# Accumulator banks of a blocked MLP: four half-used banks packed in two, four banks for first products, the output chain on DVE, eight products for the last two items

## The chip, the cores and the metric

The kernel runs on one core of one Trainium2 chip. A core has five engines that run their own instruction streams and wait for each other by semaphores: TensorE (PE in the profile; its weight loads are PEld), VectorE (DVE), ScalarE (ACT), GpSimd (POOL) and SyncE (SP), which here only issues DMAs. The metric is device time in microseconds (us) of one execution; lower is better. Before the change it is 464.85 us, the median of three runs (464.08 to 465.17).

## The reference: what is computed

One block of a network over x of 2048 rows (tokens) by 512 columns. A small conditioning vector c gives six modulation rows (shift, scale and gate for each half). In numpy's words, cut to what matters:

```
mod = (silu(c) @ w_mod).reshape(1, 6, 1, 512)
sa, ca, ga, sb, cb, gb = mod[:, 0], ..., mod[:, 5]
h = layernorm(x) * (1 + ca) + sa
x = x + ga * irfft2(rfft2(h) * (w_r + 1j * w_i))
h = layernorm(x) * (1 + cb) + sb
a = mish(h @ w1 + b1)                  # 512 -> 1376, mish(z) = z * tanh(softplus(z))
x = x + gb * (a @ w2)                  # 1376 -> 512
```

The change is in the last three lines, the MLP, which takes the last two thirds of the kernel's time. All is float32; the products on TensorE run on float32 numbers that are split in a high and a low part.

## The kernel before, in words

**Stages.** The kernel first does the spectral part: forward transform, multiplication by the filter, backward transform (the functions p1_..., p2_..., p3_...). The backward transform's last step, p3_row, adds its result to x, which stays in SBUF as 16 tiles of 128 rows. While that loop (s from 0 to 16) runs, w1 and parts of w2 are loaded and split, and the statistics for the second layernorm are taken tile by tile (norm_sums). norm_scale turns the statistics of four tiles into 1/std by a logarithm and an exponential on ACT and four short steps on DVE.

**The MLP's items.** The 2048 rows are 8 blocks (NB) of 256 rows, and the 1376 hidden columns are cut in 6 items per block (NT): item 0 has one tile of 96 hidden columns, items 1 to 5 have two tiles of 128 each. There are so 48 items, numbered s in the code. For each:

- up: first products. Each tile of hidden columns fills one PSUM bank of 128 x 512 floats, by four products 512 wide (L722) and four 256 wide (L724).
- mish: ACT adds the bias to one half of the bank (L732) and DVE adds the other half (L733); this add is the bank's last reader. Then comes Mish on ACT (L735). For a two-tile item DVE forms four sums and differences (L745), since the second products use a scheme of seven instead of eight products for two halves of rows by two halves of hidden columns.
- high and low: the seven operands are rounded to their high part on ACT (L755, two casts) and the rest is taken on DVE (L761, two subtractions).
- down: second products. Seven products of 256 columns, each as three matmuls (high by high, high by low, low by high; TERMS), so 21 matmuls (L784); item 0 has six matmuls 512 wide (L770). They add up over the items of a block.

down lags two items behind (LAG): TensorE's order is up(s), transposes if any, down(s - 2). The order on every engine is the order in which the program's text issues the instructions (tc.manual_schedule).

**Banks.** PSUM has eight banks here, as four names (A, B, C, D) of two. First products of the MLP take A (two banks), so tile one of item s waits until the add L733 of item s - 1 has read its bank. The transposes of the next block's rows (transpose_in, in items 4 and 5) also take A. The six sums of a block take C, B, B, C, D, D; the tables RAW, SUM and END say which product goes into which bank and half. Four of these six banks use only 256 of 512 columns.

**Output chain.** After the block's last down, in item 1 of the next block, gather copies the four half-used banks to SBUF with ACT (L791). own_rows reads the two full banks with DVE (L796, L797). chain then combines these on POOL (L802 to L819: five additions and two products by the gate gb), add_rows adds them to x on POOL (L824), and store writes two tiles with one DMA each. In the last block the chain runs on DVE and the last item uses plain eight products, whose w2 tile is loaded anew and split by plain_w2.

**Next block's rows.** norm_pair normalizes two tiles on ACT in item 3 (L141), transpose_in turns them in items 4 and 5, and split_in scales, rounds (ACT, L624, L628) and subtracts (DVE, L629). The next block's first products need all of it.

Of the kernel before, what the change touches and what calls it, by code (L numbers as in the profile page):

```python
# [23 lines left out]
RAW = ((0, None, 0, 0), (1, 0, 2, 1), (2, 0, 1, 6))  # L24
SUM = ((3, None, 3, 3), (4, None, 4, 4), (5, None, 5, 5), (1, 1, 6, 2))
# [5 lines left out]
def tile_spectral_block(ctx: ExitStack, tc: tile.TileContext, x_d, w1_d, b1_d, w2_d,  # L31
# [668 lines left out]
    def plain_w2():  # L700
        w2["plain"] = [w.rearrange("p e d -> p (e d)") for w in w2[1]]
        h, l = w2["plain"]
        for e, r in enumerate(st.pop(("w2", 5))):
            split(h[:, 512 * e:512 * e + 512], l[:, 512 * e:512 * e + 512], r)
# [9 lines left out]
    def up(g):  # L714
# [3 lines left out]
        for e, f, rows in tiles(t):  # L718
            ps = bank("C" if g < 2 and e == 0 else "A")[:rows]
# [7 lines left out]
    def mish(g):  # L727
# [9 lines left out]
        if g == total - 1:  # L737
# [25 lines left out]
    def down(g):  # L763
        b, t = divmod(g, NT)
        a = acts.pop(g)
        if t == 0:
            out_ps[b] = out = [bank(n) for n in "CBBCDD"]
# [5 lines left out]
        if g == total - 1:  # L773
            for n, half in ((2, 0), (1, 1)):
                for f in range(2):
                    for i, (p, q) in enumerate(TERMS):
                        nc.tensor.matmul(out[n], a[p][:, half + 2 * f], w2["plain"][q][:, 512 * f:512 * f + 512],
                                         start=False, stop=(f == 1 and i == 2))
            return
        for n, half, e, r in END if g == total - 2 else RAW + SUM:  # L780
            o = out[n][:, 0:256] if half is None else out[n][:, 256 * half:256 * half + 256]
            last = t == 5 or (half is None and g == total - 2)
            for i, (p, q) in enumerate(TERMS):
                nc.tensor.matmul(o, a[p][:, e], w2[t][q][:, r], start=(half is None and t == 1 and i == 0),  # L784
                                 stop=(last and i == 2 and (n, half) != (1, 0)))

    def gather(b):
        out = out_ps[b]
        p, q = buf("h"), buf("h")
        for o, k in ((p[:, 0:256], 0), (q[:, 0:256], 4), (q[:, 256:], 5), (p[:, 256:], 3)):  # L790
            nc.scalar.copy(o, out[k][:, 0:256])  # L791
        done[b] = p, q

    def own_rows(b):
        r = buf("y"), buf("y")
        nc.vector.tensor_tensor(r[1], out_ps[b][1], done[b][0], op=ALU.add)  # L796
        nc.vector.tensor_copy(r[0], out_ps[b][2])  # L797
        return r

    def chain(b, eng, r):  # L800
        p, q = done.pop(b)
        eng.tensor_tensor(q[:, 0:256], q[:, 0:256], p[:, 0:256], op=ALU.add)  # L802
        eng.tensor_tensor(q[:, 256:], q[:, 256:], q[:, 0:256], op=ALU.add)
        both = q[:, 256:].unsqueeze(1).to_broadcast([P, 2, 256])
        v = r[0].rearrange("p (j d) -> p j d", j=2)
        if b == NB - 1:
            eng.tensor_copy(v, both)
        else:
            eng.tensor_tensor(v, v, both, op=ALU.add)
        eng.tensor_tensor(r[0][:, 256:], r[0][:, 256:], p[:, 256:], op=ALU.add)  # L810
        if b == NB - 1:
            eng.tensor_tensor(r[1][:, 256:], p[:, 256:], q[:, 0:256], op=ALU.add)
            eng.tensor_tensor(r[1][:, 0:256], p[:, 0:256], gbr[:, 0:256], op=ALU.mult)
            eng.tensor_tensor(r[1][:, 256:], r[1][:, 256:], gbr[:, 256:], op=ALU.mult)
            eng.tensor_tensor(r[0], r[0], gbr, op=ALU.mult)
        else:
            eng.tensor_tensor(r[1][:, 256:], r[1][:, 256:], q[:, 0:256], op=ALU.add)
            for t in r[::-1]:
                eng.tensor_tensor(t, t, gbr, op=ALU.mult)  # L819

    def add_rows(b, eng, r, rows=(1, 0)):
        for i in rows:
            n = 2 * b + i
            eng.tensor_tensor(x[:, n, :], x[:, n, :], r[i], op=ALU.add)  # L824

    def store(b, rows=(1, 0)):
        for r in rows:
            n = 2 * b + r
            nc.sync.dma_start(ov[:, n:n + 1, :], x[:, n:n + 1, :])
# [4 lines left out]
    def mlp(s):  # L834
# [20 lines left out]

    def finish():
        b = NB - 1
        down(total - 2)
        gather(b)
        r = buf("y"), buf("y")  # L860
        chain(b, nc.vector, r)
        add_rows(b, nc.vector, r)
        down(total - 1)
        for i in range(2):
            nc.vector.tensor_tensor(r[i], out_ps[b][2 - i], gbr, op=ALU.mult)
            add_rows(b, nc.vector, r, (i,))
            store(b, (i,))
# [8 lines left out]
    for s in range(N2 + 1):  # L876
# [26 lines left out]
        if s in (7, 8):  # L903
            split_in(0, s - 7)
    low(high(0, mish(0)))
# [4 lines left out]
    for s in range(LAG, total):  # L910
# [9 lines left out]
        if s == 2 * NT + 2:  # L920
# [142 lines left out]
```

## Time and profile before

| | |
|---|---|
| median of three runs | 464.85 us (464.08 to 465.17) |
| profiled execution | 464.28 us, of which the span of the trace is 462.5 |
| busy, share of the span | PE 88%, PEld 80%, DVE 68%, ACT 56%, POOL 35% |
| mean granted TensorE clock | 0.966 |
| MLP's first product | at 154.26 us |
| last product | ends at 455.58 us |

A row of the timeline has the start, the duration, the engine, the line and the operation, the tile written and the tiles read, the shapes and how many instructions are merged (x4). A bracket gives the idle time of that engine before it and the instruction that ended it. A row of the windows has, for each engine, the busy time and the number of instructions, then the TensorE clock that was granted (1.00 is full speed), the share of DMA and GB/s. A group of the lines has the busy time in all, the mean of one in ns, and the idle time before. L numbers are lines of the kernel before.

### The profile page before, as it was taken

To read this page: it belongs to the slowest core of one execution; us is meant where nothing else is said; L and a number is where in the kernel's file an instruction comes from. 1 tells how busy PE (TensorE), PEld (TensorE's weight loads), DVE (VectorE), ACT (ScalarE), POOL (GpSimd) and SP (SyncE) were. 2 spreads that over 40 slices of the span, in tenths; PEclk is the share of its full clock that TensorE was granted. 3 is DMA by queue.
4 is the path that set the end of the run, shared out by engine and by line. 5 is a ranking of instruction groups with operands and counts; after the bars stand their busy time and mean duration, and the time that the engine had idled before them with its cause. 6 is when DMAs were issued, how large, how long until landed. Compare 5 with 4: busy or idle time off the path is not lost.

```text
span 462.5 us, 7587 instructions
## 1 busy us (share of the span) xinstructions
PE 407.9 (88%) x2800; PEld 369.5 (80%) x2800; DVE 312.8 (68%) x620; ACT 259.5 (56%) x563; POOL 159.6 (35%) x188
## 2 busy tenths in 40 slices
PE   8999899999999997978985997998798799699694
PEld 7888678998999887867874985887787688688593
DVE  2999786862899867585466539547655764853966
ACT  1778646666496576636547643653654464464261
POOL 0776446560566122080053008007104302600800
PEclk9999999999999999997998899899899899999998
DMA  8999814622134101000001000000100100100111
GB/s 278 354 345 327 300 58 133 247 79 91 50 120 123 40 26 46 1 22 24 0 1 46 1 0 30 18 1 0 47 1 1 45 1 0 47 0 1 39 54 45
DMA packets 20900, 35.21 MB, mean 76 GB/s; under 512 B 3712, under 2 KB 6560, under 8 KB 20480
## 3 DMA queue, kind: packets, MB, share of 16 engines
q1 hardware_dynamic: 20432, 34.21, 21.8%
q10 hardware_dynamic: 432, 0.53, 0.3%
q8 instruction: 22, 0.36, 0.3%
q14 instruction: 14, 0.11, 0.1%
HBM read 30.53 MB, written 4.19 MB: 75 GB/s over the span
## 4 chain that ended last, share of the span: by engine, by line
PE 44%; DVE 32%; ACT 16%; issue 4%; DMA 2%; POOL 1%; SPq 0%; DVEq 0%; ACTq 0%; POOLq 0%
PE bank L784 12%; PE bank L722 12%; PE bank L724 6%; DVE buf L745 5%; DVE al L761 4%; DVE st L112 4%; ACT ah L755 3%; DVE buf L733 3%; PE bank L456 3%; PE bank L502 2%; DVE ve L125 2%; ACT buf L735 2%; ACT buf L141 2%; DVE x L650 2%; ACT buf L791 2%
## 5 line engine op out<-in xcount | busy, mean ns | idle before, releaser
L745 DVE TENSOR_TENSOR buf<-buf 128x128 f32<-128x128 f32 x156 | 62.5, 441 | 29.4 <-ACT buf L735 27.4
L761 DVE TENSOR_TENSOR al<-buf,ah 128x512 fp32r<-128x512 f32 (+2 forms) x87 | 65.5, 779 | 18.1 <-ACT ah L755 15.8
L755 ACT CAST ah<-buf 128x512 fp32r<-128x512 f32 (+2 forms) x87 | 46.0, 550 | 46.8 <-DVE buf L745 32.1
L722 PE MATMUL bank<-h2e,w1h 128*128 128x512 f32 (+1 forms) x176 | 53.3, 424 | 18.0 <-DVE buf L733 16.4
L722 PE MATMUL bank<-h2o,w1h 128*128 128x512 f32 (+1 forms) x176 | 53.3, 423 | 17.7 <-DVE buf L733 15.4
L802 POOL TENSOR_TENSOR buf<-buf 128x256 f32<-128x256 f32 x7 | 5.2, 744 | 183.1 <-ACT buf L791 183.1
L732 ACT ACTIVATE buf<-bank,b1n 128x256 f32<-128x256 f32 (+1 forms) x88 | 40.4, 472 | 43.7 <-PE bank L724 43.7
L733 DVE TENSOR_TENSOR buf<-buf,bank 128x256 f32<-128x256 f32 (+1 forms) x88 | 35.3, 416 | 38.6 <-ACT buf L732 38.4
L735 ACT ACTIVATE buf<-buf 128x512 f32<-128x512 f32 (+1 forms) x48 | 28.6, 597 | 44.7 <-DVE buf L733 44.6
L722 PEld LDWEIGHTS bank<-h2e,w1h 128*128 128x128 f32 (+1 forms) x176 | 31.6, 199 | 26.1 <-DVE buf L733 18.9
L722 PEld LDWEIGHTS bank<-h2o,w1h 128*128 128x128 f32 (+1 forms) x176 | 31.5, 199 | 26.1 <-DVE buf L733 18.0
L784 PE MATMUL bank<-w2a,ah 128*128 128x256 f32 x168 | 36.9, 286 | 0.0
L784 PE MATMUL bank<-w2b,ah 128*128 128x256 f32 x161 | 34.3, 283 | 0.0
L724 PEld LDWEIGHTS bank<-h2o,w1l 128*128 128x128 f32 (+1 forms) x176 | 29.1, 202 | 4.5
L724 PEld LDWEIGHTS bank<-h2e,w1l 128*128 128x128 f32 (+1 forms) x176 | 29.0, 201 | 4.6
L724 PE MATMUL bank<-h2o,w1l 128*128 128x256 f32 (+1 forms) x176 | 30.1, 297 | 0.0
L724 PE MATMUL bank<-h2e,w1l 128*128 128x256 f32 (+1 forms) x176 | 30.0, 296 | 0.0
L784 PEld LDWEIGHTS bank<-w2a,ah 128*128 128x128 f32 x168 | 28.1, 192 | 0.0
L784 PEld LDWEIGHTS bank<-w2b,ah 128*128 128x128 f32 x161 | 26.8, 191 | 0.0
L112 DVE BATCH_NORM_STATS2 st<-x 128x6 f32<-128x512 f32 x32 | 22.0, 688 | 4.9 <-DMA x<-in_A_x_dram 4.5
L637 PE MATMUL bank<-kc,d 128*128 128x128 f32 x128 | 24.8, 276 | 0.5 <-ACT d L360 0.5
L234 PE MATMUL bank<-buf,mring 128*128 128x512 f32 x48 | 21.4, 446 | 4.2 <-DVE buf L227 1.9
(210 smaller groups left out, 1054.7 us busy)
## 6 DMA issues: line engine op xcount, KB each, us to landing
buf<-in_B_w_dram SPq DMA_DIRECT2D x20, 256.0 KB, 2.7
xring<-in_x_t_dram SPq DMA_DIRECT2D x16, 256.0 KB, 4.8
x<-in_A_x_dram SPq DMA_DIRECT2D x16, 256.0 KB, 5.1
wm<-in_w_mod_dram SPq DMA_DIRECT2D x16, 256.0 KB, 4.3
out_dram<-x SPq DMA_DIRECT2D x16, 256.0 KB, 2.0
mraw<-in_km_dram SPq DMA_DIRECT2D x16, 128.0 KB, 4.9
wqa<-in_w_q_dram SPq DMA_DIRECT2D x8, 256.0 KB, 4.3
wqb<-in_w_q_dram SPq DMA_DIRECT2D x8, 256.0 KB, 4.6
```

What stands on the lines that cost most here:

```text
L112: nc.vector.bn_stats(t, x[:, n, :])
L234: nc.tensor.matmul(pa, m[:, a, 0:128], g, start=(i == 0), stop=False)
L637: nc.tensor.matmul(o, dj[:, 0:128], kc[0][:, n, :], start=True, stop=False)
L722: nc.tensor.matmul(ps, w1h[:, k, fs], h[:, k], start=(k == 0), stop=False)
L724: nc.tensor.matmul(ps[:, 0:256], w1l[:, k, fs], h[:, k, 0], start=False, stop=(k == 3))
L732: nc.scalar.activation(o, ps[:, 256:], AF.Identity, bias=b1n[:rows, f:f + 1])
L733: nc.vector.tensor_tensor(o, o, ps[:, 0:256], op=ALU.add)
L735: nc.scalar.activation(o, o, AF.Mish)
L745: nc.vector.tensor_tensor(o, p, q, op=op)
L755: nc.scalar.copy(h, r)
L761: nc.vector.tensor_tensor(l, r, h, op=ALU.subtract)
L784: nc.tensor.matmul(o, a[p][:, e], w2[t][q][:, r], start=(half is None and t == 1 and i == 0), stop=(last and i == 2 and (n, half) != (1, 0)))
```

## The change

- The four half-used sums share two banks: sums 0 and 3 are two halves of one bank, 4 and 5 of another. A block's sums take C, B, B, C. Only the first product into such a bank carries the start flag.
- First products take A for an item's first tile and D for its second, so four banks in turn; the transposes take A and D likewise (items of the first block before it: C and D).
- In item 1 of a block the order becomes up, Mish, down of the last block's item 5, gather (two copies 512 wide), then the casts of high; before, the casts came ahead of gather.
- The output chain runs on DVE: four steps (chain) ahead of low's subtractions and four (residual) behind them, the last two 1024 wide over both tiles; POOL has nothing of it. One DMA stores both tiles.
- norm_scale of the last four tiles moves from item 2 of block 2 to just ahead of the first Mish.
- The last two items, not one, use eight plain products; their w2 tiles are loaded anew (two more DMAs) and split into the places of w2 items 1 and 2. down_last runs the 24 products 512 wide for both items at the end, the even rows' bank first. finish combines the block's other sums on ACT, DVE and POOL while they run.

```diff
-RAW = ((0, None, 0, 0), (1, 0, 2, 1), (2, 0, 1, 6))
-SUM = ((3, None, 3, 3), (4, None, 4, 4), (5, None, 5, 5), (1, 1, 6, 2))
+RAW = ((0, 0, 0, 0), (1, 0, 2, 1), (2, 0, 1, 6))
+SUM = ((0, 1, 3, 3), (3, 0, 4, 4), (3, 1, 5, 5), (1, 1, 6, 2))
...
-        st["pt2", g] = ps = bank("A" if n else "D")
+        st["pt2", g] = ps = bank("AD"[g] if n else "D")
...
-            ps = bank("C" if g < 2 and e == 0 else "A")[:rows]
+            ps = bank("CD"[e] if g < 2 else "AD"[e])[:rows]
...
-        if g == total - 1:
+        if g >= total - 2:
             parts = [(w, slice(0, 4))]
...
-            out_ps[b] = out = [bank(n) for n in "CBBCDD"]
+            out_ps[b] = out = [bank(n) for n in "CBBC"]
...
+    def down_last():
+        out = out_ps[NB - 1]
+        for n, half in ((2, 0), (1, 1)):
+            for g in (total - 2, total - 1):
                 for f in range(2):
                     for i, (p, q) in enumerate(TERMS):
+                        nc.tensor.matmul(out[n], acts[g][p][:, half + 2 * f],
+                                         w2["plain", g % NT][q][:, 512 * f:512 * f + 512],
+                                         start=False, stop=(g == total - 1 and f == 1 and i == 2))
...
+    rows = modr[:, 0:2]
     def gather(b):
         out = out_ps[b]
         p, q = buf("h"), buf("h")
-        for o, k in ((p[:, 0:256], 0), (q[:, 0:256], 4), (q[:, 256:], 5), (p[:, 256:], 3)):
-            nc.scalar.copy(o, out[k][:, 0:256])
+        nc.scalar.copy(p, out[0])
+        nc.scalar.copy(q, out[3])
         done[b] = p, q
...
+    def chain(b):
+        p, q = done[b]
+        nc.vector.tensor_tensor(rows[:, 1], out_ps[b][1], p, op=ALU.add)
+        nc.vector.tensor_tensor(q[:, 0:256], q[:, 0:256], p[:, 0:256], op=ALU.add)
+        nc.vector.tensor_tensor(q[:, 256:], q[:, 256:], q[:, 0:256], op=ALU.add)
+        both = q[:, 256:].unsqueeze(1).to_broadcast([P, 2, 256])
+        nc.vector.tensor_tensor(rows[:, 0].rearrange("p (j d) -> p j d", j=2),
+                                out_ps[b][2].rearrange("p (j d) -> p j d", j=2), both, op=ALU.add)
+
+    def residual(b):
         p, q = done.pop(b)
+        nc.vector.tensor_tensor(rows[:, 1, 256:], rows[:, 1, 256:], q[:, 0:256], op=ALU.add)
+        nc.vector.tensor_tensor(rows[:, 0, 256:], rows[:, 0, 256:], p[:, 256:], op=ALU.add)
+        nc.vector.tensor_tensor(rows, rows, gbr.unsqueeze(1).to_broadcast([P, 2, D]), op=ALU.mult)
+        xb = x[:, 2 * b:2 * b + 2, :]
+        nc.vector.tensor_tensor(xb, xb, rows, op=ALU.add)
+        nc.sync.dma_start(ov[:, 2 * b:2 * b + 2, :], xb)
...
+        if t == 1 and b:
+            down(s - LAG)
+            gather(b - 1)
         parts = high(s, parts)
-        down(s - LAG)
+        if t != 1 or not b:
+            down(s - LAG)
         if t == 1 and b:
-            gather(b - 1)
-            r = own_rows(b - 1)
+            chain(b - 1)
         low(parts)
         if t == 1 and b:
-            chain(b - 1, nc.gpsimd, r)
-            add_rows(b - 1, nc.gpsimd, r)
-            store(b - 1)
+            residual(b - 1)
...
+        nc.gpsimd.tensor_tensor(u, u, gbr, op=ALU.mult)
+        down_last()
...
+        nc.gpsimd.tensor_tensor(xu, xu, u, op=ALU.add)
...
+    norm_scale(N2 - 4, N2)
     low(high(0, mish(0)))
...
-        if s == 2 * NT + 2:
-            norm_scale(N2 - 4, N2)
-        if s == total - 5:
+        if s == total - 4:
+            load_w2(4)
+        if s == total - 3:
+            plain_w2(4)
             load_w2(5)
-        if s == total - 3:
-            plain_w2()
+        if s == total - 2:
+            plain_w2(5)
```

More of the change, by code (lines that the diff above doesn't have):

```diff
@@ L698, in split_w2, with plain_w2 @@
             split(h[:, 256:768], l[:, 256:768], v)
[L700 to L703, printed above, removed]
+    def plain_w2(t):
+        h, l = w2["plain", t] = [w.rearrange("p e d -> p (e d)") for w in w2[t - 3]]
+        for e, r in enumerate(st.pop(("w2", t))):
             split(h[:, 512 * e:512 * e + 512], l[:, 512 * e:512 * e + 512], r)
@@ L821, in add_rows @@
[L821 to L829, printed above, removed]
+    def chain(b):
[6 more added lines that the diff above has]
+                                out_ps[b][2].rearrange("p (j d) -> p j d", j=2), both, op=ALU.add)
```

69 lines of the change are left out of this document (24 added, 45 removed).

## The prediction

> **What bounds the kernel now.** I read the page first (engine totals, then the costliest groups with the idle time before them), then the timeline of TensorE alone, then DVE and POOL at one block's start, then the windows for the clock.
>
> ```profile
> span 462.5 us, 7587 instructions
> ...
> PE 407.9 (88%) x2800; PEld 369.5 (80%) x2800; DVE 312.8 (68%) x620; ACT 259.5 (56%) x563; POOL 159.6 (35%) x188
> ...
> L722 PE MATMUL bank<-h2e,w1h 128*128 128x512 f32 (+1 forms) x176 | 53.3, 424 | 18.0 <-DVE buf L733 16.4
> ```
>
> The last row says where TensorE stands still: before a first product, until the DVE add of L733 has emptied a bank. The timeline gives the places (h2e is an even block, h2o an odd one):
>
> ```profile
> 186.55 0.70 PE L722 MATMUL bank<-h2o,w1h 128*96 128x512 f32 x2 [0.56 <-DVE h2o L629]
> ...
> 251.53 2.07 PE L722 MATMUL bank<-h2e,w1h 128*128 128x512 f32 x4 [5.65 <-DVE buf L733]
> ...
> 266.71 0.70 PE L722 MATMUL bank<-h2o,w1h 128*96 128x512 f32 x2 [0.56 <-DVE h2o L629]
> ...
> 304.20 0.70 PE L722 MATMUL bank<-h2e,w1h 128*96 128x512 f32 x2 [0.57 <-DVE h2e L629]
> ...
> 307.72 1.09 PE L722 MATMUL bank<-h2e,w1h 128*128 128x512 f32 x4
> ...
> 309.12 1.11 PE L722 MATMUL bank<-h2e,w1h 128*128 128x512 f32 x4
> ...
> 313.04 1.09 PE L722 MATMUL bank<-h2e,w1h 128*128 128x512 f32 x4
> ...
> 319.21 1.19 PE L722 MATMUL bank<-h2e,w1h 128*128 128x512 f32 x4 [1.40 <-DVE buf L733]
> ...
> 327.33 1.20 PE L722 MATMUL bank<-h2e,w1h 128*128 128x512 f32 x4 [2.53 <-DVE buf L733]
> ...
> 416.69 0.71 PE L722 MATMUL bank<-h2o,w1h 128*96 128x512 f32 x2 [0.57 <-DVE h2o L629]
> ...
> 439.44 1.19 PE L722 MATMUL bank<-h2o,w1h 128*128 128x512 f32 x4 [2.13 <-DVE buf L733]
> ```
>
> A block runs from one 0.56 row to the next: 80.2 us for the second and third together (186.55 to 266.71), then 37.5 each (266.71 to 416.69 is four). One tile of first products takes 309.12 - 307.72 = 1.40; a tile and an item of second products take 313.04 - 309.12 = 3.92, so the 21 second products take 2.5. A block's TensorE work is 11 tiles (15.4), five items (12.6), the 96-row item (six products as long as a tile's 512-wide ones, 1.4) and two transposes (0.7): 30.1. So 7.4 of 37.5 are lost: 0.57 + 1.40 + 2.53 shown idle, about 1.2 in overlaps that the idle figure leaves out, and the rest in the clock:
>
> ```profile
> 210.00:212.00 2.00, 2.00 (x7) 1.62 (x7) 1.33 (x5) 1.42 (x3) 0.00 (x0) 0.50 0.03 8
> 212.00:214.00 2.00, 2.00 (x7) 1.68 (x7) 1.24 (x3) 0.78 (x2) 0.00 (x0) 0.50 0.00 0
> 328.00:330.00 2.00, 2.00 (x10) 1.71 (x9) 1.46 (x5) 1.42 (x4) 0.00 (x0) 0.62 0.00 0
> 330.00:332.00 2.00, 2.00 (x9) 1.80 (x8) 1.02 (x2) 0.47 (x3) 0.00 (x0) 0.52 0.00 0
> 440.00:442.00 2.00, 2.00 (x13) 1.74 (x12) 1.46 (x5) 1.43 (x4) 0.00 (x0) 1.00 0.59 221
> ```
>
> After the 2.53 wait of 327.33 the granted clock is 0.62 and 0.52 for 4 us: (0.38 + 0.48) x 2 = 1.7 us lost. After the 2.13 wait of 439.44 it stays 1.00. The waits themselves come from DVE beside POOL:
>
> ```profile
> 320.19 2.74 POOL L819 TENSOR_TENSOR buf<-buf,modr 128x512 f32<-128x512 f32 x2
> 322.90 2.63 POOL L824 TENSOR_TENSOR x<-x,buf 128x512 f32<-128x512 f32 x2
> ```
>
> ```profile
> 315.39 0.69 DVE L796 TENSOR_TENSOR buf<-bank,buf 128x512 f32<-128x512 f32 x1 [2.02 <-ACT buf L791]
> 316.00 0.68 DVE L797 COPY buf<-bank 128x512 f32<-128x512 f32 x1
> 316.60 2.23 DVE L761 TENSOR_TENSOR al<-buf,ah 128x384 fp32r<-128x384 f32 x2
> 318.75 0.74 DVE L733 TENSOR_TENSOR buf<-buf,bank 128x256 f32<-128x256 f32 x2
> 320.19 4.20 DVE L745 TENSOR_TENSOR buf<-buf 128x128 f32<-128x128 f32 x4 [0.70 <-ACT buf L735]
> 324.31 2.23 DVE L761 TENSOR_TENSOR al<-buf,ah 128x384 fp32r<-128x384 f32 x2
> 326.85 0.79 DVE L733 TENSOR_TENSOR buf<-buf,bank 128x256 f32<-128x256 f32 x2 [0.31 <-ACT buf L732]
> 328.34 1.02 DVE L745 TENSOR_TENSOR buf<-buf 128x128 f32<-128x128 f32 x4 [0.70 <-ACT buf L735]
> 329.28 0.55 DVE L761 TENSOR_TENSOR al<-buf,ah 128x384 fp32r<-128x384 f32 x1
> 330.04 0.69 DVE L761 TENSOR_TENSOR al<-buf,ah 128x512 fp32r<-128x512 f32 x1 [0.21 <-ACT ah L755]
> ```
>
> While POOL runs the output chain, L745 takes 4.20 for what takes 1.02 after it, and the L761 pair 2.23 instead of 1.2; L733, which reads a bank, keeps 0.74. That is 3.2 + 1.0 + 1.0 = 5.2 us of DVE time per block.
>
> **The change, part by part.** *Chain on DVE.* It removes two DVE instructions (0.69 + 0.68), all POOL work of the blocks and, I take it, the 5.2. It adds eight on DVE, priced by these rows and L796:
>
> ```profile
> L810 DVE TENSOR_TENSOR buf<-buf 128x256 f32<-128x256 f32 x1 | 0.4, 426 | 0.1
> ...
> L685 DVE TENSOR_TENSOR w<-modr,w 128x1024 fp32r<-128x1024 f32 x1 | 1.2, 1192 | 0.0
> ...
> 324.95 1.51 ACT L141 ACTIVATE buf<-x,nmr,rstd 128x512 f32<-128x512 f32 x2
> ...
> 327.67 0.63 ACT L735 ACTIVATE buf<-buf 128x512 f32<-128x512 f32 x1 [0.49 <-DVE buf L733]
> ```
>
> Two 512-wide with a bank (0.69), four 256-wide (0.42), two 1024-wide (1.2; twice 0.69 is the other end): 5.5, with gaps between dependent ones about 6.0. DVE's sum per block falls by 0.6, but the chain now stands in front of item 2's adds. Two 512-wide ACT copies replace four 256-wide ones over the same elements; I count them alike, 0.6 each.
>
> *Four banks.* An item's tiles no longer wait for the item before, but for the one two before. I lay the rows out from the end of a block's last second products (time 0). TensorE: item 2 until 2.8, the 96-row second products until 4.2, item 3 until 7.0, second products until 9.5, item 4 until 12.3. DVE: copies at 0.1 and 0.6, chain from 0.8 to 3.1 (the B banks are free by then, the 96-row products do not wait), L761 of item 1 until 4.2, residual until 7.4. Only now come item 2's adds (7.8 and 8.1), Mish to 8.8, L745 to 9.9, its second cast to 10.5, the norm pair on ACT to 12.0, item 3's adds at 12.8. Transposes of item 4 need a bank whose reader is item 3's add: a wait of 0.4. Item 4's adds end at 16.5, TensorE is at item 5 by 15.7: 0.9. Item 5's Mish ends at 21.9; the scaling, cast and subtraction of its transposes (1.0 + 0.62 + 0.69) end at 24.2, TensorE needs them at 22.7: 1.5. Sum 2.8, so a block takes 32.9 (33 below) instead of 37.5. The waits on L733 that held 1.40 and 2.53 vanish; the one on L629 grows from 0.6 to some 1.3 shown idle. As 2.13 at 439.44 left the clock at 1.00, I expect no drop from it.
>
> *Rstd of the last four tiles* moves from the third block to the start.
>
> ```profile
> 246.14 1.28 ACT L117 ACT_TABLE_LOAD   x1
> ...
> 158.40 0.18 DVE L113 BATCH_NORM_AGGREGATE mv<-st 128x2 f32<-128x6 f32 x1
> ...
> 158.91 0.42 ACT L735 ACTIVATE buf<-buf 96x256 f32<-96x256 f32 x1 [1.12 <-DVE buf L733]
> ```
>
> The third block loses three such loads (3.8 on ACT) and the 5.65 wait: it becomes a 33 like the others. At the start ACT must wait for L113 until 158.6, then take its two small steps, a bias and the load that Mish needs anyway (1.28): Mish 2 us later than at 158.91. TensorE has the four banks to fill meanwhile, so of these 2 us nothing need show before the first block's end. I let the head gain 1 by the waits on banks that go (ends: 2 lost, 3 gained).
>
> *Eight products for the last two items.* 12 products 512 wide take 2.8 instead of 2.5 (+0.3); DVE drops L745 and half an L761 (1.5, hidden). Two more 256 KB loads go into SP's queue behind the last block's store, which waits for the residual; the ACT casts that need the second load are at its landing with the last item's biases behind them: 0.8 lost, ends 0 and 2. The stores become seven of 512 KB; nobody waits for them.
>
> *Tail.*
>
> ```profile
> 455.19 0.39 PE L777 MATMUL bank<-w,al 128*128 128x512 f32 x1
> ...
> 458.51 0.69 DVE L824 TENSOR_TENSOR x<-x,buf 128x512 f32<-128x512 f32 x1
> ```
>
> From the last product to the last add now 3.6 (DVE is still in its chain); after, two 0.69 steps and gaps, about 2. POOL's two finishing products run beside two-input DVE steps, which by the 4.20 row costs up to 2; I take 1. Tail -0.6 in all.
>
> **Sum.** Head -1; 186.55 to 266.71: 80.2 to 33 + 33 and 0.8 that I leave for the last weight splits, which lie there, -13.4; four blocks 150.0 to 132, -18; 416.69 to the end 45.8: waits of 1.4 and 2.13 with overlaps -4, tail -0.6, products and load +1.1, -3.5. At the first block's end the wait on L629 carries the 2 us of the late start on top of its 0.6, more than 2.53: half clock once, +1.7. Together -34.2: the profiled execution of 464.28 becomes 430.1; the median of the runs shown, 464.85, is 0.57 higher, so I say 430.5.
>
> **Rivals.** *The waits at a block's end vanish too*, if DVE's steps overlap more than I let them: 6 x 2.8 less, 414. For it: ACT and DVE are busy for only 56% and 68% of the span. Against it: they run one after the other within an item. *Half clock after the 1.5 wait at each block's end*: 1.7 x 6 = 10, 441. For it: 2.53 was enough; against it: 2.13 was not.
>
> By the Trainium skill's page TensorE: Matmul & The Clock Gate, Part 1, only an idle window of about 3.4 us throttles; the 2.53 of 327.33 contradicts it, and by that rule this rival would be void, with the sum unchanged.
>
> *Slower*: the three waits that I leave in a block (0.4, 0.9, 1.5) are short but recur every few us, and each is followed by half clock as in the two rows at 0.50 (4 us, 2 lost): 3 x 2 x 7 = 42, so 473. It decides from 34 / 7 = 4.9 us per block on, that is only if nearly every wait trips the clock. For it: the half clock of those rows lasted longer than any wait of the block; against: the 1.00 after 2.13.
>
> The same page, section A second HAM failure mode, describes this: cycling through banks with micro-idles makes the clock oscillate; no row of this trace shows it for waits under 2 us.
>
> *POOL is not what slows DVE*: 4.20 and 2.23 stay, item 2 is later by 3.2 + 2 behind the longer chain, a block stays 37.5, and only the third block, head and end gain some 9: 455. Against it: the long rows (to 326.5) stop within 1 us of POOL's last (to 325.5).
>
> **How the numbers follow.** Forecast 0.60 (range 423 to 439); waits vanish 0.12; half clock at block ends 0.17; POOL not the cause 0.06; slower 0.05. The middle 8 in 10 run from the first rival to beyond the second: 415 to 447. A measurement of this kernel tells 0.2% (1 us) from none; only the slower rival and the fringe of the fourth end there: faster 0.94, same 0.01, slower 0.05.
>
> **What would show it.** Blocks 33 apart; L745 at 1.0 and L761 at 1.2 after the chain; no wait before the first products of items 3 and 4, some 0.7 shown idle at item 5 and 1.3 on the h2 subtraction; PEclk 1.0 between blocks; no table load in the third block. I am wrong if the chain's 1024-wide steps take far over 1.2, if TensorE waits for B or C banks after the copies, or if the clock drops at each block's end.

## The result and the profile after

The changed kernel takes 427.11 us (median, 426.62 to 429.21), the kernel before beside it on the same chip 464.47 (463.7 to 465.17): a ratio of 0.920, interval 0.917 to 0.924. The forecast was 430.5, with 415 to 447 as its range. The profiled execution took 427.04 us, of which the trace spans 425.2.

From the page of the changed kernel: its span, busy times, and the two groups of first products (one line each for even and odd blocks; after the bar busy time, mean ns, idle before). Line numbers shift: L721 is now the first product, L732 the DVE add that empties its bank, L744 the four small sums, L760 the two subtractions, L801 to L814 the output chain.

```profile
span 425.2 us, 7487 instructions
...
PE 394.4 (93%) x2791; PEld 360.6 (85%) x2791; DVE 300.6 (71%) x654; ACT 253.3 (60%) x546; POOL 91.1 (21%) x127
...
L721 PE MATMUL bank<-h2e,w1h 128*128 128x512 f32 (+1 forms) x176 | 50.6, 407 | 8.7 <-DVE h2e L629 4.4
...
L721 PE MATMUL bank<-h2o,w1h 128*128 128x512 f32 (+1 forms) x176 | 49.5, 399 | 6.9 <-DVE h2o L629 5.6
```

The even group stood idle for 18.0 us before the change, 16.4 of it behind the DVE add (the odd one for 17.7, with 15.4 behind it); now it is 8.7, and half of what is left (4.4; 5.6 of 6.9 in the odd blocks) ends with the h2 subtraction at a block's end. TensorE is busy for 93% of a shorter span instead of 88%. The timeline of TensorE alone has the places:

```profile
178.54 2.07 PE L721 MATMUL bank<-h2e,w1h 128*128 128x512 f32 x4 [2.94 <-DVE buf L732]
...
187.55 0.70 PE L721 MATMUL bank<-h2o,w1h 128*96 128x512 f32 x2 [1.11 <-DVE h2o L629]
...
244.91 1.19 PE L721 MATMUL bank<-h2e,w1h 128*128 128x512 f32 x4 [0.44 <-DVE buf L732]
...
252.89 0.70 PE L721 MATMUL bank<-h2o,w1h 128*96 128x512 f32 x2 [1.51 <-DVE h2o L629]
...
383.57 0.71 PE L721 MATMUL bank<-h2o,w1h 128*96 128x512 f32 x2 [1.48 <-DVE h2o L629]
...
414.73 0.73 PE L786 MATMUL bank<-w2a,ah 128*128 128x512 f32 x2 [0.61 <-ACT ah L754]
```

Stretch by stretch, measured against the sum of the prediction: the start to 187.55 lost 1.0 (186.55 before); from there to 252.89 are 65.3 for the second and third block (80.2 before); to 383.57 are 130.7 for four blocks, 32.67 each (37.5 before); from there to the end of the span 41.6 (45.8 before). In a block two waits are left, 0.44 at item 5 and 1.5 on the h2 subtraction; none stands at items 3 and 4. The granted clock is full through four blocks, as a window of them shows (0.94 in the same window of the kernel before):

```profile
252.00:384.00 132.00, 123.46 (x830) 111.97 (x831) 87.18 (x211) 77.64 (x155) 0.00 (x0) 1.00 0.04 17
```

One block start on DVE, from its timeline:

```profile
262.01 0.69 DVE L801 TENSOR_TENSOR modr<-bank,buf 128x512 f32<-128x512 f32 x1
262.62 0.41 DVE L802 TENSOR_TENSOR buf<-buf 128x256 f32<-128x256 f32 x1
...
263.53 0.69 DVE L805 TENSOR_TENSOR modr<-bank,buf 128x512 f32<-128x512 f32 x1
264.13 1.15 DVE L760 TENSOR_TENSOR al<-buf,ah 128x384 fp32r<-128x384 f32 x2
265.20 0.42 DVE L810 TENSOR_TENSOR modr<-modr,buf 128x256 f32<-128x256 f32 x1
...
265.99 1.23 DVE L812 TENSOR_TENSOR modr<-modr 128x1024 f32<-128x1024 f32 x1
267.25 1.23 DVE L814 TENSOR_TENSOR x<-x,modr 128x1024 f32<-128x1024 f32 x1
268.39 0.75 DVE L732 TENSOR_TENSOR buf<-buf,bank 128x256 f32<-128x256 f32 x2
269.84 1.02 DVE L744 TENSOR_TENSOR buf<-buf 128x128 f32<-128x128 f32 x4 [0.70 <-ACT buf L734]
```

The chain's eight steps (two of 0.69, four of 0.41 to 0.43, two of 1.23) take 5.5 us here, as priced; the pair L760 is back from 2.23 to 1.15 and the four sums from 4.20 to 1.02. Item 2's adds (268.39) come only behind the last step of the chain, and TensorE doesn't mind, since it is busy with item 3 in the other two banks by then.

### The profile page after: what moved, and what is told of

Read it like the earlier page. It is cut to its first block, busy times and chain, and to the rows that moved or that the text cites. A ratio compares the mean times of both kernels' runs of the same rounds, so it can differ in the third digit from the quotient of the medians.

```text
span 425.2 us, 7487 instructions
## 1 busy us (share of the span) xinstructions
PE 394.4 (93%) x2791; PEld 360.6 (85%) x2791; DVE 300.6 (71%) x654; ACT 253.3 (60%) x546; POOL 91.1 (21%) x127
## 4 chain that ended last, share of the span: by engine, by line
DVE 40%; PE 25%; ACT 19%; issue 6%; DMA 5%; POOL 3%; SPq 0%; POOLq 0%; DVEq 0%; ACTq 0%
PE bank L721 6%; DVE buf L744 6%; DVE buf L732 5%; ACT buf L734 5%; DVE al L760 5%; PE bank L777 4%; DMA buf<-in_B_w_dram 4%; PE bank L723 3%; DVE st L112 3%; PE bank L456 3%; PE bank L502 3%; ACT ah L754 3%; ACT buf L141 2%; DVE ve L125 2%; ACT buf L624 2%
## 5 line engine op out<-in xcount | busy, mean ns | idle before, releaser
L760 DVE TENSOR_TENSOR al<-buf,ah 128x512 fp32r<-128x512 f32 (+2 forms) x86 | 50.1, 603 | 20.6 <-ACT ah L754 20.6
L744 DVE TENSOR_TENSOR buf<-buf 128x128 f32<-128x128 f32 x152 | 39.8, 303 | 28.2 <-ACT buf L734 25.8
L721 PE MATMUL bank<-h2e,w1h 128*128 128x512 f32 (+1 forms) x176 | 50.6, 407 | 8.7 <-DVE h2e L629 4.4
L721 PE MATMUL bank<-h2o,w1h 128*128 128x512 f32 (+1 forms) x176 | 49.5, 399 | 6.9 <-DVE h2o L629 5.6
L731 ACT ACTIVATE buf<-bank,b1n 128x256 f32<-128x256 f32 (+1 forms) x88 | 38.5, 467 | 28.2 <-PE bank L723 28.2
L732 DVE TENSOR_TENSOR buf<-buf,bank 128x256 f32<-128x256 f32 (+1 forms) x88 | 34.0, 416 | 26.2 <-ACT buf L731 26.2
L721 PEld LDWEIGHTS bank<-h2e,w1h 128*128 128x128 f32 (+1 forms) x176 | 30.5, 191 | 15.1 <-DVE h2e L629 5.8
L721 PEld LDWEIGHTS bank<-h2o,w1h 128*128 128x128 f32 (+1 forms) x176 | 29.8, 187 | 13.2 <-DVE h2o L629 7.4
L777 PE MATMUL bank<-w2b,ah 128*128 128x256 f32 x147 | 31.8, 283 | 0.0
L723 PEld LDWEIGHTS bank<-h2e,w1l 128*128 128x128 f32 (+1 forms) x176 | 27.2, 189 | 4.2
L723 PEld LDWEIGHTS bank<-h2o,w1l 128*128 128x128 f32 (+1 forms) x176 | 26.7, 185 | 4.1
L723 PE MATMUL bank<-h2o,w1l 128*128 128x256 f32 (+1 forms) x176 | 27.8, 280 | 0.0
L637 PE MATMUL bank<-kc,d 128*128 128x128 f32 x128 | 24.9, 276 | 0.5 <-ACT d L360 0.5
L638 PE MATMUL bank<-kc,d 128*128 128x128 f32 x128 | 24.7, 275 | 0.0
```

Source lines behind the costliest of these rows:

```text
L637: nc.tensor.matmul(o, dj[:, 0:128], kc[0][:, n, :], start=True, stop=False)
L638: nc.tensor.matmul(o, dj[:, 64:192], kc[1][:, n, :], start=False, stop=True)
L721: nc.tensor.matmul(ps, w1h[:, k, fs], h[:, k], start=(k == 0), stop=False)
L723: nc.tensor.matmul(ps[:, 0:256], w1l[:, k, fs], h[:, k, 0], start=False, stop=(k == 3))
L731: nc.scalar.activation(o, ps[:, 256:], AF.Identity, bias=b1n[:rows, f:f + 1])
L732: nc.vector.tensor_tensor(o, o, ps[:, 0:256], op=ALU.add)
```

## Experiments

Medians are those of each kernel; the ratios are to the kernel before on the same chip, whose own median moved between 464.5 and 469.4 from chip to chip. Where two kernels weren't run on one chip, their traces are compared, each of one execution.

### The chain on DVE alone, with the banks of before

```diff
-            chain(b - 1, nc.gpsimd, r)
-            add_rows(b - 1, nc.gpsimd, r)
+            chain(b - 1, nc.vector, r)
+            add_rows(b - 1, nc.vector, r)
```

> The kernel before with one part of the change alone: the output chain and the row adds on DVE instead of POOL; two banks for first products as before. My theory is that POOL slows DVE, and that the gain of 37 us needs the four banks as well, because the chain on DVE stands in front of item 2's adds: L745 and the L761 pair after the chain fall back from 4.20 and 2.23 to about 1.0 and 1.2, but some 8 us of chain on DVE (ten steps of 0.42 to 0.69, four of them the x adds and products) come before item 2's adds, and with two banks TensorE must wait for them: one wait of 5 to 6 us on the first-product add in each block in place of 1.40 and 2.53. Block 37 to 38, time 462 to 472. Rival: POOL's slowing of DVE is the whole cause and the banks give nothing: a block falls to 33 and the time to about 435.

Measured: 474.36 us against 465.58, ratio 1.018 (1.016 to 1.021): slower by some 2%, and 2 us beyond the range that was expected. Timeline of DVE, of TensorE, and a window of this kernel (its lines are those of before):

```profile
287.59 1.02 DVE L745 TENSOR_TENSOR buf<-buf 128x128 f32<-128x128 f32 x4 [0.69 <-ACT buf L735]
```

```profile
286.62 2.07 PE L722 MATMUL bank<-h2o,w1h 128*128 128x512 f32 x4 [5.20 <-DVE buf L733]
```

```profile
288.00:290.00 2.00, 2.00 (x8) 1.74 (x7) 1.77 (x5) 1.45 (x4) 0.00 (x0) 0.50 0.05 12
```

DVE is as fast as hoped (L745 takes 1.02), and still the kernel loses. Item 2's adds now stand behind the whole chain, TensorE has only two banks and waits 5.20 for them, and behind that wait it runs at half clock. A block takes 38.95 us (267.88 to 423.66 is four) instead of 37.5. Of the 1.45 more, some 0.6 is the clock, by an estimate from the windows of four blocks: half clock lasts 6.83 us in each here and 3.41 before the change, and the products that run in it fill 4.7 and 3.4 us, half of which is lost. So freeing DVE from POOL is worth nothing by itself.

### The chain back on POOL, with the four banks

```diff
-        nc.vector.tensor_tensor(q[:, 0:256], q[:, 0:256], p[:, 0:256], op=ALU.add)
...
+        nc.vector.tensor_copy(rows[:, 0], out_ps[b][2])
...
+        eng = nc.gpsimd
+        eng.tensor_tensor(q[:, 0:256], q[:, 0:256], p[:, 0:256], op=ALU.add)
...
+            eng.tensor_tensor(rows[:, i], rows[:, i], gbr, op=ALU.mult)
...
+            eng.tensor_tensor(xb[:, i], xb[:, i], rows[:, i], op=ALU.add)
```

> The changed kernel with one part undone: the steps of the output chain that touch no bank (the three 256-wide sums that stay, the spread of q over row 0, the gate products and the x adds) go back to POOL; DVE keeps the add of bank B and a copy of the other. If POOL slows DVE as in the trace before (L745 4.20 for 1.02, the L761 pair 2.23 for 1.2), DVE is free 5 us earlier for item 2's adds but loses 5 to 6 us over the next two items: block 33 to 35, time 427 to 440, and L744 shows 3 to 4.5 us. Rival (POOL does not slow DVE, the order of the chain alone set the time before): L744 stays at 1.02, the waits at the end of a block go, block 31, time 415 to 418.

Measured: 432.64 us (430.85 to 434.01), ratio 0.929 (0.925 to 0.933). DVE beside POOL, and TensorE's wait at the block's end, from the timelines:

```profile
263.85 2.68 DVE L760 TENSOR_TENSOR al<-buf,ah 128x384 fp32r<-128x384 f32 x2
266.45 0.74 DVE L732 TENSOR_TENSOR buf<-buf,bank 128x256 f32<-128x256 f32 x2
267.89 4.21 DVE L744 TENSOR_TENSOR buf<-buf 128x128 f32<-128x128 f32 x4 [0.70 <-ACT buf L734]
272.02 2.25 DVE L760 TENSOR_TENSOR al<-buf,ah 128x384 fp32r<-128x384 f32 x2
```

```profile
267.90 2.75 POOL L815 TENSOR_TENSOR modr<-modr 128x512 f32<-128x512 f32 x2
```

```profile
253.50 0.70 PE L721 MATMUL bank<-h2o,w1h 128*96 128x512 f32 x2 [1.48 <-DVE h2o L629]
...
286.80 0.71 PE L721 MATMUL bank<-h2e,w1h 128*96 128x512 f32 x2 [1.48 <-DVE h2e L629]
```

POOL does slow DVE, by the same figures as before the change (4.21 for 1.02 on the four sums; L732, which reads a bank, keeps 0.74). But the block is 33.30 us (253.50 to 286.80) instead of 37.5, with the chain on POOL and DVE as slow as before; the changed kernel's is only 0.63 shorter. DVE is busy for 312.9 us in all here and 300.6 in the changed kernel, 1.8 per chain: for DVE the chain of its own costs nearly what POOL's slowing costs. With the run above this makes four corners: both parts old 465.6, the chain moved alone 474.4, the banks (with the rest of the change) 432.6, everything 427.1. So the gain doesn't hang on the engine of the chain; the chain on DVE turns from a loss of 9 into a gain once the rest is there, of 3.8 by the spans of the traces (429.0 and 425.2) and 5.5 by the medians.

What these corners don't separate is the banks from the new place of gather ahead of the casts, which is in this kernel too. Item 2's adds come 12.95 us after the block's first products here (253.50 to 266.45), and 14.55 before the change (304.20 to 318.75), since DVE no longer waits 2.02 for the copies. An estimate from these rows: with two banks and gather moved, the adds of items 2 and 3 and the products behind them would each come 1.6 earlier, so of the 4.2 us by which a block is shorter here, 1.6 belongs to gather and the rest to the banks. No run has either alone.

### Rstd of the last four tiles back in the third block

```diff
-    norm_scale(N2 - 4, N2)
...
+        if s == 2 * NT + 2:
+            norm_scale(N2 - 4, N2)
```

> The changed kernel with the rstd of the last four tiles back in the third block. My sum gave that move: third block 41.4 to 33 in the kernel before, of which the three activation-table loads are 3 x 1.28 = 3.8 and the rest came with the wait on a bank of 5.65. With four banks a part of the wait is covered: I expect the third block 3.5 to 5 longer, the head 1 to 2 shorter, so 429 to 432, and a half clock of 1.7 on top if a wait there passes 2.5. Rival: the banks cover the table loads wholly, third block unchanged, 425 to 427. Other rival: the whole 8.4 comes back, 434.

Measured: 430.25 us (428.78 to 430.7), ratio 0.924 (0.921 to 0.926). The third block, on ACT and on TensorE:

```profile
236.68 1.28 ACT L117 ACT_TABLE_LOAD   x1
```

```profile
242.07 0.66 PE L616 MATMUL bank<-ident,buf 128*128 128x128 f32 x4 [2.70 <-DVE buf L732]
...
254.65 0.71 PE L721 MATMUL bank<-h2o,w1h 128*96 128x512 f32 x2 [1.51 <-DVE h2o L629]
```

The three table loads are back (the first is shown; the others start at 238.29 and 241.94), and with them a wait of 2.70 on a bank. The third block takes 36.6 (218.04 to 254.65) for 32.7, so the move is worth 3.9 there, about the three loads; the head is 2.2 shorter without it (185.38 for 187.55). By the traces the move brings 1.8 us, by the medians 3.1, with ratios whose intervals overlap; two of the four executions had a mean clock of 0.985 where the profiled one had 0.994, so a further drop of the clock is a likely part of the difference.

### Eight products for the last item alone

```diff
-        if g >= total - 2:
+        if g == total - 1:
...
-        for n, half, e, r in END if g == total - 3 else RAW + SUM:
+        for n, half, e, r in END if g == total - 2 else RAW + SUM:
...
-        if s == total - 4:
-            load_w2(4)
+        if s == total - 5:
+            load_w2(5)
```

> The changed kernel with eight products for the last item alone, as the kernel before had it; the item before it by seven again. My sum put eight products for two items at +0.3 for the products and +0.8 for the second load, its DVE saving hidden: then undoing half of it makes the kernel faster by up to 1.1, 426.0 to 427. Rival: DVE's saved sums and subtraction (1.5) are on the path at the end, and the time rises by 1 to 1.5: 428 to 429.

Measured: 426.46 us (425.96 to 427.26), ratio 0.908 (0.906 to 0.911). In absolute time this is 0.65 below the changed kernel, but on another chip and with overlapping runs, so a gain isn't established. In the traces the last block's start agrees (383.58 and 383.57), and the last add on DVE starts at 421.09 instead of 421.46: eight products for the item before last cost 0.4.

### The residual behind items 2 and 3

```diff
+    def gate_rows(b):
         nc.vector.tensor_tensor(rows, rows, gbr.unsqueeze(1).to_broadcast([P, 2, D]), op=ALU.mult)
+
+    def add_rows(b):
         xb = x[:, 2 * b:2 * b + 2, :]
...
+        if t == 2 and b:
+            gate_rows(b - 1)
+        if t == 3 and b:
+            add_rows(b - 1)
```

> The changed kernel with the last two steps of the residual moved on DVE: the gate product (1024 wide) behind item 2's work and the x add with the store behind item 3's, instead of both ahead of item 2's adds. My hand schedule says that the waits left at a block's end (0.43 before the transposes, 1.48 on the h2 subtraction in the trace) come from item 2's adds being late behind the residual: then the 1.48 falls to some 0.5, the 0.43 goes, the blocks fall from 32.67 to 31, time 416 to 420. Rival: these waits come from ACT and DVE running one after the other within an item, so that the two steps only move: blocks stay at 32.5 to 32.7, time 426 to 428.

Measured: 420.07 us (418.67 to 421.38), ratio 0.901 (0.898 to 0.904). TensorE's waits:

```profile
179.28 1.21 PE L721 MATMUL bank<-h2e,w1h 128*128 128x512 f32 x4 [2.93 <-DVE buf L732]
188.34 1.17 PE L721 MATMUL bank<-h2o,w1h 128*96 128x512 f32 x2 [2.57 <-DVE h2o L629]
...
252.22 0.71 PE L721 MATMUL bank<-h2o,w1h 128*96 128x512 f32 x2 [0.80 <-DVE h2o L629]
...
377.40 0.71 PE L721 MATMUL bank<-h2o,w1h 128*96 128x512 f32 x2 [0.79 <-DVE h2o L629]
```

The wait at item 5 is gone and the one on the h2 subtraction is 0.80 instead of 1.5; a block takes 31.30 (252.22 to 377.40 is four). So of the two waits that the change left, the first and half of the second came from item 2's adds standing behind the residual, as the hand schedule had it.

### Weight splits of the first block spread

The kernel above, with pair 4's splits half behind item 3 and half behind item 4, and pair 5's half behind item 5 and half behind the next block's item 0:

```diff
             split_w2(4, False)
+        if s == 4:
             split_w2(4, True)
             load_w2(5)
             sum_w2(5, 0, 1, 2, 3)
         if s == 5:
             split_w2(5, False)
+        if s == 6:
             split_w2(5, True)
```

> The kernel with the residual behind items 2 and 3, and also with the weight splits of the first block spread: those of pair 4 half after item 3 and half after item 4, those of pair 5 half after item 5 and half after the 96-row item of the next block, instead of two whole pairs after items 3 and 5. My reading of the trace is that the 2.94 wait of the first block (and one half clock behind it) comes from four casts and four subtractions, 4.2 us, in front of item 4's adds. Then the wait falls under 1.5, the half clock of the first block goes, and the time falls by 2 to 4 from 420.1: 416 to 418. Rival: the wait is set by the late start of the block, and the splits only move it: 419 to 421.

Measured: 419.21 us (418.58 to 420.54), ratio 0.899 (0.895 to 0.902), an interval that overlaps with the one of the kernel above. TensorE's waits in the first block:

```profile
177.29 1.19 PE L721 MATMUL bank<-h2e,w1h 128*128 128x512 f32 x4 [1.56 <-DVE buf L732]
187.03 0.69 PE L721 MATMUL bank<-h2o,w1h 128*96 128x512 f32 x2 [3.28 <-DVE h2o L629]
```

The rival holds: the wait of 2.93 in the first block falls to 1.56, and the next one, on the h2 subtraction, rises from 2.57 to 3.28. The half clock of the first block is gone from this trace, a matter of its own (below), and the second block's first products start 1.3 earlier (187.03 for 188.34).

### The second transposes ahead of item 5's first products

```diff
-        up(s)
-        if t in (4, 5) and nxt:
+        early = t in (5,) and nxt
+        if early:
+            transpose_in(nxt, t - 4)
+            split_in(nxt, t - 4)
+        up(s)
+        if t in (4, 5) and nxt and not early:
             transpose_in(nxt, t - 4)
...
-        if t in (4, 5) and nxt:
+        if t in (4, 5) and nxt and not early:
             split_in(nxt, t - 4)
```

> The same with the second pair of transposes of a block, and what ACT and DVE do for it, ahead of item 5's first products instead of behind them. The wait that the spread residual left at the end of a block is 0.79 on the h2 subtraction: if it comes from ACT's scaling and cast standing behind item 5's biases and Mish, it goes, a block falls from 31.3 to 30.5 to 30.7, and the time by another 4 to 5: 412 to 414. Rival: transposes ahead of the first products must wait for the tiles of item 4's norm or for a bank, and a wait of the same size stands there: unchanged within 1.

Measured: 411.43 us (410.38 to 411.53), ratio 0.881 (0.877 to 0.885), somewhat more than was expected. The first products of two odd blocks, which now start without a wait:

```profile
245.54 1.10 PE L721 MATMUL bank<-h2o,w1h 128*96 128x512 f32 x4
...
366.64 1.10 PE L721 MATMUL bank<-h2o,w1h 128*96 128x512 f32 x4
```

The wait on the h2 subtraction is gone from the second block on, and a block takes 30.27 us (245.54 to 366.64 is four). That is nearly the TensorE work of 30.1 that the prediction counted from its rows. In the first block the wait is still there, but 1.04 instead of 3.28.

### The last weight load early

The kernel above, with the second load of plain rows issued together with the first, into two buffers that are free there:

```diff
-    def load_w2(t):
+    def load_w2(t, ring="y"):
...
-            r = buf("y")[:rows]
+            r = buf(ring)[:rows]
...
-            load_w2(4)
+            load_w2(4)
+            load_w2(5, "h")
         if s == total - 3:
             plain_w2(4)
-            load_w2(5)
```

> The kernel with the transposes first, the spread residual and splits (411.4), and with the second load of plain rows for the last items issued with the first, into the two h buffers that are free there, instead of behind the first's subtraction and the last store but one. In its trace ACT waits 1.93 for that load and the last products 1.51 for the casts behind it. If the load sets the last item, 1.2 to 1.9 go: 409.5 to 410.2. Rival: the wait only passes to the last item's own chain of adds, Mish and cast, which runs beside the load: unchanged within 0.5.

Measured: 409.40 us (409.03 to 410.4), ratio 0.872 (0.869 to 0.874), the fastest of all. Its windows:

```profile
252.00:384.00 132.00, 132.00 (x897) 121.51 (x897) 92.79 (x229) 83.28 (x164) 0.00 (x0) 1.00 0.07 25
```

From 252 to 384 us TensorE doesn't stop at all at full clock: what is left of these blocks is its own work. At the end neither ACT's wait for the load nor the wait of 1.51 before the last products is there any more.

### A longer wait at every block's end

The changed kernel, with one cast on ACT ahead of the h2 subtraction done twice, and in a second kernel three times:

```diff
-        nc.scalar.copy(hh, tv)
+        for _ in range(1 + (1 if g else 0)):
+            nc.scalar.copy(hh, tv)
```

> The changed kernel with the cast of L628 for the second pair of transposes of each block done twice (0.62 on ACT, the same values): the wait on the h2 subtraction, 1.48 in the trace, becomes some 2.1. Without any drop of the clock this costs 7 x 0.65 = 4.6 us, 431.7. What makes the clock drop is in question. Theory of the grid: in the runs so far every drop begins a whole multiple of 3.413 us after another one of the same run, and the stretch of 3.413 us before it held 1.9 us of idle TensorE or more, while stretches with up to 1.77 of idle were not followed by one (two drops after 1.33 and 1.44 of idle stand against it, both with 96-row products in the stretch). Then it counts how the wait lies on the grid: a wait of 2.1 lies with 1.85 or more in one stretch about half the time, so some 3 of 7 blocks drop, 1.7 us each: 435 to 439. Rival, by the length of the wait alone (2.13 did not in the kernel before, 2.53 did): no drop, 431 to 433. Other rival: a longer wait costs nothing, 427.

> The same with the cast done three times: the wait becomes some 2.75, without a drop 7 x 1.3 = 9.1 us, 436.2. Theory of the grid: a wait of 2.75 has 1.85 or more in one stretch of 3.413 in about 7 of 10 positions, so 4 to 6 of 7 blocks drop and the others don't: 443 to 447, with drops a multiple of 3.413 apart. Rival, by the length of the wait alone: all seven drop, 448. Other rival: none drop, 436.

Measured: 437.25 us (434.92 to 440.25), ratio 0.937 (0.932 to 0.943), and 443.38 us (440.34 to 444.32), ratio 0.949 (0.944 to 0.954). Both times lie in what the grid would give, and above the rival without a drop (431 to 433, 436); the second lies below the rival with seven drops (448). The numbers of drops were not met: five of seven waits in the first kernel's trace, where some three were expected (this execution, of 440.25 us, is the slowest of its four), and three of seven in the second's, where four to six were. What decides is the place of each drop in the first trace. Two of its waits (TensorE's timeline), and the windows that end and begin at the grid's points, 3.413 us apart (line numbers are one higher there):

```profile
224.01 1.01 PE L722 MATMUL bank<-h2e,w1h 128*96 128x512 f32 x2 [2.13 <-DVE h2e L630]
...
258.82 0.71 PE L722 MATMUL bank<-h2o,w1h 128*96 128x512 f32 x2 [2.12 <-DVE h2o L630]
```

```profile
220.80:224.21 3.41, 1.28 (x9) 0.82 (x8) 1.93 (x6) 3.30 (x7) 0.00 (x0) 1.00 0.00 0
224.21:227.62 3.41, 3.41 (x16) 3.11 (x16) 1.23 (x3) 0.89 (x2) 0.00 (x0) 0.50 0.00 0
254.94:258.35 3.41, 1.76 (x13) 1.30 (x12) 1.49 (x6) 3.08 (x6) 0.00 (x0) 1.00 0.00 0
258.35:261.76 3.41, 2.94 (x22) 2.79 (x23) 1.91 (x4) 1.52 (x4) 0.00 (x0) 1.00 0.00 0
```

Two waits of one length (2.13 and 2.12) end differently. The first lies wholly in one stretch, which is left with 1.28 of TensorE work in 3.41 (2.13 idle), and the next stretch runs at 0.50. The second is cut by a point of the grid: 1.65 idle in the first stretch, 0.47 in the next, and the clock stays at 1.00. After the first block's end, which drops behind a wait of 1.80, four of the six waits of 2.1 are followed by a drop and two aren't; a block with a drop takes 34.81 (224.01 to 258.82), one without 33.33 (258.82 to 292.15), so a drop costs 1.48. With three casts three of the seven waits are followed by a drop, and the four in between, all of 2.77 to 2.79, by none: that block takes 33.97, close to ten stretches (34.13), so its waits lie at nearly the same place on the grid block after block.

## Why the prediction was right

The forecast came out 3.4 us too high. Its mechanism held in the blocks, which carry most of the gain; in the head (the start up to the second block) it was right in sum by luck. Point by point:

- *Head* (-1, and +1.7 of half clock: +0.7): +1.0, for other reasons. Mish starts at 160.24, 1.3 later than before instead of 2. The half clock was put at the first block's end, behind a wait on the h2 subtraction over 2.53. That wait is only 1.11; the half clock came one wait earlier, behind the 2.94 at 178.54 (the first products there take 2.07 instead of 1.19), where item 4's adds stand behind the weight splits of pair 4. The prediction passed over that place, though the kernel before waits there too:

```profile
176.60 0.66 PE L616 MATMUL bank<-ident,buf 128*128 128x128 f32 x4 [2.71 <-DVE buf L733]
```

  And by the trace the half clock cost nothing there. The chain of work that ended last (rows of start, duration, engine, tile written and line) reaches the second block's first products without TensorE, through ACT, DVE, POOL and a load, from 158 us on; its end in the changed kernel is:

```profile
178.15 0.67 DVE buf L732 x2
...
186.80 0.70 DVE h2o L629
...
187.55 0.70 PE bank L721 x2
```

  So of the terms "2 lost, 3 gained" and +1.7, the first was about right (2.2, by the run with the rstd late), the last was not paid, and the gain was not 3 but 1.2; the last two errors nearly cancel. The weight splits were put at 0.8 in the second and third block; these two blocks lose nothing to them (65.3 is twice 32.67).
- *Blocks* (33 each): 32.67. Of the three waits left in the hand schedule, 0.4 at item 4 is not there, 0.9 at item 5 (0.7 shown) is 0.44, and 1.5 at the end (1.3 shown) is 1.48. The pure work of 30.1 was confirmed by the kernel whose TensorE no longer waits there (30.27). The hand schedule holds nearly step by step: counted from 261.74, its time 0, item 2's adds end at 7.4 (8.1 in the schedule) and TensorE goes on behind the h2 subtraction at 23.8 (24.2).
- *The third block's loads*: the last table load on ACT is now the one at 158.95, and the third block is a 32.7 like the others, as said. That the whole 8.4 of that block was credited without asking how much the banks alone would take was harmless for the sum; the run without the move shows 3.9 for it.
- *End* (-3.5): -4.2. Eight products for two items were put at +0.3 and +0.8 for the load; the run with one such item shows 0.4 for both. The load itself was seen rightly:

```profile
411.36 0.62 ACT L684 CAST w2a<-buf 128x512 fp32r<-128x512 f32 x1 [0.74 <-DMA buf<-in_B_w_dram]
```

  ACT waits 0.74 for it and TensorE 0.61 for the cast behind it (414.73), but part of that is covered. The product on POOL beside DVE costs 1.0, as taken: the 256-wide sum beside it takes 1.39 instead of 0.42.

```profile
416.71 1.34 POOL L854 TENSOR_TENSOR modr<-modr 128x512 f32<-128x512 f32 x1 [234.65 <-DVE modr L851]
```

```profile
416.94 1.39 DVE L853 TENSOR_TENSOR modr<-modr,buf 128x256 f32<-128x256 f32 x1
```

What carried the prediction is the schedule laid out by hand: it asked when item 2's adds would come, not how busy DVE is. It didn't ask what the new place of gather gives by itself, and no run shows that. One reading beside it didn't hold. The prediction said that the waits of 1.40 and 2.53 "come from DVE beside POOL". With that slowing fully there and four banks the block is 33.3, and without it and with two banks 38.95. POOL's share was to make DVE late, a chain on DVE makes it later still, and with a pair of banks, which ties TensorE to DVE's order within one item, either of them costs time. The rival priced at 455, in which DVE stays slow with the chain on it as well, did not come up: in the blocks DVE's steps were at full speed as soon as POOL was idle.

Of the rivals, the waits that vanish too (414) needed the residual moved (420.1) and the transposes moved (411.4): the change alone doesn't do it. Half clock at every block's end (441) and the slower rival (473), both built on waits of 1.5 and less that trip the clock, did not come either: the clock is 1.00 from 252 to 384 us with five waits of 1.5 in it, and the runs with longer waits show why (last section).

## What to carry to other kernels

When an engine waits for another through a buffer, count how many items ahead it may run before asking what the other engine spends: here four banks instead of two, with gather moved up, made late adds harmless, while moving work off a slow neighbour lost time as long as there were two. Then place work that nobody waits for (the residual) behind the work that somebody waits for, also on an engine that is idle a quarter of the time; that and an earlier place for the transposes brought some 16 us more, with the spread splits. And price a wait near 2 us with both outcomes of the clock: the same wait is free of it or costs 1.5 us, by where it falls, if the slowed products are on the path at all; in the changed kernel's first block they weren't.

## What the runs showed of the hardware

*The clock's grid.* In each trace all beginnings of half clock during the MLP lie whole multiples of 3.413 us apart, where there are several (in the kernel with the cast done twice 3, 10, 20, 20 and 10 of them). What decides is the idle time within one such stretch: in the MLP, stretches with 1.65 to 1.78 us idle were not followed by a drop (eight cases), and those with 1.80 or more were. This explains what the prediction had to weigh as a puzzle. The wait of 2.13 in the kernel before is cut by the grid of its run:

```profile
437.71:441.13 3.42, 1.70 (x9) 1.51 (x10) 2.69 (x7) 1.73 (x4) 0.32 (x1) 1.00 0.77 274
441.13:444.54 3.41, 3.41 (x27) 3.25 (x26) 3.19 (x8) 2.40 (x5) 0.00 (x0) 1.00 0.06 21
```

1.72 of it falls in the stretch from 437.71, the other 0.41 before, and the clock stays. In the kernel with the spread splits even a wait of 3.28 passes (its grid is counted back from its one drop, at 413.95, behind the last product):

```profile
181.84:185.25 3.41, 1.91 (x15) 1.45 (x13) 2.68 (x5) 2.16 (x6) 2.15 (x3) 1.00 0.01 2
185.25:188.67 3.42, 1.64 (x12) 1.51 (x13) 3.42 (x8) 2.87 (x6) 0.77 (x2) 1.00 0.02 5
188.67:192.08 3.41, 3.41 (x27) 3.23 (x26) 1.06 (x3) 1.81 (x4) 0.00 (x0) 1.00 0.00 0
```

The Trainium skill's page TensorE: Matmul & The Clock Gate, Part 1, calls the window free-running and 3413 ns long; the spacing of the drops agrees. It lets the clock fall after an idle window; here a window about half idle is enough. The prediction said that by that rule its sum would be unchanged; its own +1.7 for a half clock would have gone as well.

In the MLP the clock came back after the first stretch at half clock in which TensorE was idle for 0.50 us or less. Where that stretch held 0.61 or more, half clock lasted a second one, 6.83 us in all: so twice in the kernel before (the wait of 5.65 is one), once with three casts, and at all seven waits of 5.2 with the chain on DVE alone.

Three cases don't fit. In the kernel with the chain on DVE alone two drops followed stretches with only 1.44 and 1.33 idle; both stretches held the second products of item 0, which use 96 rows. Whether such products count for less wasn't tried. And 1.83 idle behind the very last product of the kernel with early transposes was not followed by a drop in the next stretch.

*DVE beside POOL.* Two-input steps from SBUF slow down as long as POOL runs, by factors of 2 to 4 (1.02 to 4.21, 1.15 to 2.25 or 2.68, 0.42 to 1.39): before the change, in the kernel with the chain back on POOL and at the changed kernel's end; a step with one operand in a bank keeps its time (0.74).
